# Column-tiled issue of the dense matmuls that stand between a score visit and the values after it

## Chip, cores and metric

The kernel runs on one core of one Trainium2 chip. The metric is device time in microseconds (us); lower is better. The time before is the median of three runs, 385.58 us.

## What is computed

Sigmoid attention (8 batches, 12 heads, 448 positions, head width 64) is followed by a two-layer network with a swish gate, on 3584 tokens of width 768 and a hidden width of 2048.

```python
scores = scale * np.matmul(q, k.transpose(0, 1, 3, 2)) - np.log(S)
attn = 1.0 / (1.0 + np.exp(-scores))
x = np.matmul(attn, v)              # then heads side by side: (3584, 768)
h = x @ w_in                        # (3584, 2048)
g = h * (1.0 / (1.0 + np.exp(-beta * h)))
out = g @ w_out                     # (3584, 768)
```

Inputs and output are float32; the kernel multiplies in fp16 and accumulates in float32.

## The kernel before

TensorE (PE) does four kinds of matmul, each in its own tiling of the 128 x 128 array:

- **Scores** (`score`, line 200): a contraction over 32 rows, so four matmuls stand in the array at once, each on its own 32 rows ("32*128" in the profile; "32*64" for the last 64 keys of a head). `visit(g, jt)` makes the scores of four heads (a group g, 24 in all) against the jt-th 128 keys, in 8 matmuls of 448 columns, and lets ScalarE (ACT) turn them into attention weights (`weigh`, line 211). The fourth visit (jt = 3, 64 keys) is made for two groups at once, with the odd group.
- **Values** (`attend`, line 266): the attention weights times v. A head fills 64 columns of the array, so two heads stand side by side ("128*64"), each streaming its own 448 columns. `attend` takes four heads as two slots of two: three pairs for the first slot, three for the second, then four matmuls in "64*64" for the last 64 keys. Each slot accumulates in a PSUM bank of its own, and VectorE (DVE) copies it to `xT` (line 275).
- **First layer** (`dense1`, line 284): six matmuls of the full array ("128*128") with 448 columns per 128 hidden units (224 columns in the opening part); then a sigmoid on ACT (line 292) and a product on DVE (line 295).
- **Second layer**: `dense2` (line 314) and `strassen` (line 396), full array, mostly 384 columns per matmul. `strassen` does two row tiles with seven products in place of eight; DVE adds up the products (line 415) and prepares sums of hidden values (line 385).

PE's work is laid out by hand. The main loop (line 607) goes through the visits of the groups from 3 on. After each visit a `while` loop (line 636) fills in "units" of dense work, of a list made beforehand, up to a budget; a visit and its filling are some 3 us. When the visits of a group are through, the next step of the loop begins with line 612, which fills a few more units if PSUM banks are held, and then calls `attend` for the finished group. So the order on PE around the end of a group is: last visit of group g, dense units, values of group g, first visit of group g+1, dense units, and so on. `spread`, `rest` and the units' costs decide only how many units stand in each place.

A matmul is two instructions on PE: a load of the stationary operand (PEld) and the matmul that streams the moving one. For a dense matmul the stationary operand is a 128 x 128 block (`w_in16` in the first layer, `gt` or `sums` in the second), the moving one is `xT` or a weight block, and the output is one PSUM bank, given by `bank`, which hands out the bank that has been out of use for longest.

Of the kernel before, what the change touches and what calls it, by code (L numbers as in the profile page):

```python
# [13 lines left out]
def kernel(  # L14
# [10 lines left out]
    nc = tc.nc  # L25
# [3 lines left out]
    B, H, S, D = q.shape  # L29
    NTOK, DM = out.shape  # L30
    DFF = moe_w_in.shape[1]
    P = 128
# [51 lines left out]
    def bank(name: str, cols: int = S, hold=None):  # L84
        i = min((i for i in used if i not in held.values()), key=used.get)
        touch(i)
        if hold is not None:
            held[hold] = i
        return psum["one"].tile([P, cols], FP32, tag=f"one{i}", name=name)
# [27 lines left out]
    def load_qk(g: int):  # L117
        load_one(g, 0)
        load_one(g, 1)
# [4 lines left out]
    def last_base(s: int) -> int:  # L124
        return (s % 2 ^ swapped(s // 2)) * KL
# [27 lines left out]
    def load_w_out(c: int, half: int):  # L153
# [4 lines left out]
            in_=moe_w_out[c * n * P : (c + 1) * n * P, cols].rearrange("(c p) f -> p c f", p=P),  # L158
        )

    qT = {}
    kT = {}
    at_tiles = {}
# [91 lines left out]
    def attend(g: int, c0: int, n: int, part=(0, 1)):  # L255
        b, t = divmod(g, QPB)
        if b not in xTs:
            xTs[b] = xTp.tile([P, NHC, S], FP16, tag="xT", name="xT")
        slots = [2 * g + x for x in part]
        avs = [bank("av_ps") for _ in slots]  # L260
        todo = [(s, av, jt) for s, av in zip(slots, avs) for jt in range(JF)]
        for s, av, jt in todo + [(s, av, JF) for s, av in zip(slots, avs)]:
            at = at_tiles.pop((s, jt, c0))
            base, nk = (last_base(s), KL) if jt == JF else (0, P)
            for hh in range(2):
                nc.tensor.matmul(  # L266
                    av[hh * D : (hh + 1) * D, 0:n],
                    vs[b][base : base + nk, 2 * (s % NPAIR) + hh, jt],
                    at[base : base + nk, hh, 0:n],
                    start=(jt == 0),  # L270
                    stop=(jt == JF),
                    tile_position=(base, hh * D),
                )
        for s, av in zip(slots, avs):
            nc.vector.tensor_copy(out=xTs[b][:, s % NPAIR, c0 : c0 + n], in_=av[:, 0:n])  # L275
# [4 lines left out]
    def dense1(b: int, dc: int, c0: int = 0, n: int = S):  # L280
        off = (b % 2) * S + c0
        m1 = bank("m1_ps")
        for hc in range(NHC):
            nc.tensor.matmul(  # L284
                m1[:, 0:n],
                w_in16[:, hc, dc * P : (dc + 1) * P],
                xTs[b][:, hc, c0 : c0 + n],
                start=(hc == 0),
                stop=(hc == NHC - 1),
            )  # L290
        sg = sigp.tile([P, S], FP32, tag="sg", name="sg")
        nc.scalar.activation(  # L292
            out=sg[:, 0:n], in_=m1[:, 0:n], func=AF.Sigmoid, bias=0.0, scale=beta_sb[:, dc : dc + 1]
        )
        nc.vector.tensor_tensor(  # L295
            out=gt[:, dc, off : off + n], in0=m1[:, 0:n], in1=sg[:, 0:n], op=ALU.mult
        )
# [4 lines left out]
    def release(key):  # L302
        touch(held.pop(key))
        m2s.pop(key)

    def dense2(t: int, half: int, part: int):
        last = t == NT - 1
        mid = 512 if last else HALF
        lo, hi = (0, mid) if half == 0 else (mid, DM)
        if part == 0:  # L310
            m2s[t, half] = bank("m2_ps", hi - lo, (t, half))
        m2 = m2s[t, half]
        for dc in range(part * NDC // N2, (part + 1) * NDC // N2):
            nc.tensor.matmul(  # L314
                m2,
                gt[:, dc, cols(t)],
                w_out16[:, dc, lo:hi],
                start=(dc == 0),
                stop=(dc == NDC - 1),
            )  # L320
        if part < N2 - 1:
            return
        release((t, half))
        if half == 0:
            osbs[t] = outp.tile([P, DM], FP32, tag="osb", name="osb")
        osb = osbs[t]
        nc.vector.tensor_copy(out=osb[:, lo:hi], in_=m2)  # L327
        if last:
            store(t, lo, hi)
        elif half == 1:  # L330
            store(t, 0, DM)
# [3 lines left out]
    def cols(t: int):  # L335
        return slice(t % NTILE * P, (t % NTILE + 1) * P)
# [44 lines left out]
    def hidden_sum(t: int, i: int):  # L381
        _, x, y, op, _ = product(t, i)
        if op is not None:
            sums[t, i] = sump.tile([P, ND, P], FP16, tag="sum", name="sum")
            nc.vector.tensor_tensor(out=sums[t, i], in0=x, in1=y, op=op)  # L385

    def strassen(t: int, i: int, part: int):
        name, x, _, op, w = product(t, i)
        if part == 0 and i + 2 < NPROD:
            hidden_sum(t, i + 2)  # L390
        first = (t, name) not in m2s
        if first:
            m2s[t, name] = bank("m2_ps", HALF, (t, name))
        m2 = m2s[t, name]
        for dc in range(part * ND // 2, (part + 1) * ND // 2):
            nc.tensor.matmul(  # L396
                m2,
                (x if op is None else sums[t, i])[:, dc],
                w[:, dc],
                start=first and dc == 0,  # L400
                stop=(dc == ND - 1),
                skip_group_check=i >= 4,
            )
            first = False if dc else first
        if part == 0:
            return
        if i == 0:
            for u in (t, t + 1):
                osbs[u] = outp.tile([P, DM], FP32, tag="osb", name="osb")
        L, R = slice(0, HALF), slice(HALF, DM)  # L410
        o1, o2 = osbs[t], osbs[t + 1]
        r, a = m2s.get((t, "r")), m2s.get((t, "a"))

        def add(out, in0, in1, op=ALU.add):
            nc.vector.tensor_tensor(out=out, in0=in0, in1=in1, op=op)  # L415

        if i == 1:
            nc.scalar.copy(out=o2[:, L], in_=a)
        elif i == 2:
            nc.vector.tensor_copy(out=o1[:, L], in_=m2)  # L420
            add(o1[:, R], r, o1[:, L])
            release((t, "s"))
        elif i == 3:
            add(o2[:, L], m2, o2[:, L])
            release((t, "b"))
        elif i == 4:
            add(o2[:, R], a, o2[:, L], ALU.subtract)
        elif i == 5:
            add(o2[:, R], r, o2[:, R])
            release((t, "r"))  # L430
            store(t + 1, 0, DM)
        elif i == 6:
            add(o1[:, L], a, o1[:, L], ALU.subtract)
            release((t, "a"))
            store(t, 0, DM)
# [50 lines left out]
    def fill_units(n: int):  # L486
        for _ in range(n):
            fill[at_fill[0]][2]()
            at_fill[0] += 1
# [4 lines left out]
    with tc.manual_schedule():  # L494
# [90 lines left out]
        visits = [(QPB, jt, ()) for jt in range(JF + 1)]  # L585
# [21 lines left out]
        for i, (g, jt, also) in enumerate(visits):  # L607
            if jt == 0:
                if g > QPB:


                    while len(held) > 1 and (len(held) > 2 or fill[at_fill[0]][3]):
                        spent += fill[at_fill[0]][0]
                        fill_units(1)
                    attend(g - 1, 0, S)
                if g + 2 < NQUAD:
                    if g + 2 not in raws:
                        load_qk(g + 2)
                if g + 1 < NQUAD and (g + 1) % QPB == 0:
                    load_v((g + 1) // QPB)  # L620
            visit(g, jt, also)
            if jt in (1, 2) and QPB < g < NQUAD - 1:
                transpose(g + 1, jt - 1)
            if jt == 2 and g % QPB == 0 and g > QPB:
                double_v_last(g // QPB)
            for name, part in adds.get(i, ()):
                weight_sum(name, part)
            budget += spread[i] if i < len(spread) else rest
            if (g, jt) == (QPB, JF):
                fill_units(3 * N2 // 4)  # L630
                spent += 3 * M2_US / 4
                transpose(g + 1, 0)
                transpose(g + 1, 1)
                double_v_last(1)
            goal = max(budget, spent + LEAST_US) if g > QPB + 2 else budget
            while at_fill[0] < len(fill):
                cost, ready, _, _ = fill[at_fill[0]]
                if ready > g or spent + cost / 2 > goal:
                    break
                spent += cost  # L640
                fill_units(1)
        attend(NQUAD - 1, 0, S)
        fill_units(len(fill) - at_fill[0])


# [28 lines left out]
```

## Time and profile before

| | us |
|---|---|
| three runs | 385.4, 385.58, 386.72 |
| the profiled execution | 385.93 |
| its span on the core | 384.2 |
| PE busy in the span | 377.9 |
| ACT busy | 229.3 |
| DVE busy | 231.9 |

The span runs from the first to the last instruction of the core; the other 1.7 us of the profiled execution lie around it. The granted TensorE clock was 1.0. In rows of the profile a line such as "PE L396 MATMUL ... 128*128 128x384 f16 x12" is read so: twelve matmuls of line 396 in the 128*128 tiling, with 384 columns streamed. Successive matmuls overlap, since the duration of one holds its way through the array; what one costs is the step from its start to the start of the next.

### The profile page before, as it was taken

The page shows a single profiled execution, that of the slowest core. Times are in us where ns is not written, and L with a number is a line of the kernel's source. Part 1 is how long each engine was busy: PE and PEld are TensorE (multiplying, and loading weights), DVE is VectorE, ACT ScalarE, POOL GpSimd, SP SyncE. Part 2 cuts the span into 40 slices and gives each one's busy share as a digit, 9 for nine tenths or more (in the row PEclk, how much of TensorE's full clock was granted, in tenths as well). Part 3 has the DMA queues.
Part 4 walks back from the last instruction along what each step waited for, and adds up shares of the span by engine and source line. Part 5 has one row for each costly group of instructions (what it writes and reads, how often), then busy time and mean ns, then how long its engine had stood idle before and what let it go on. Part 6 is the DMA issues. An engine that isn't in the chain of part 4 may idle for free.

```text
span 384.2 us, 7371 instructions
## 1 busy us (share of the span) xinstructions
PE 377.9 (98%) x2987; PEld 190.6 (50%) x2987; DVE 231.9 (60%) x439; ACT 229.3 (60%) x330; POOL 66.4 (17%) x114
## 2 busy tenths in 40 slices
PE   8999999999999999999999999999999999999996
PEld 3478744444544444444554445544455444555563
DVE  3347366775765557555774657665675665655761
ACT  5987856697355776487355782477752787535200
POOL 7833343140110410040110410113100000000000
PEclk9999999999999999999999999999999999999999
DMA  9999999845363930572363750649203300030033
GB/s 166 171 197 204 197 205 212 166 67 58 49 130 84 120 50 2 130 95 26 49 130 84 97 74 2 131 88 116 49 0 84 84 1 2 0 84 0 0 84 123
DMA packets 42401, 34.64 MB, mean 90 GB/s; under 512 B 21872, under 2 KB 38656, under 8 KB 42368
## 3 DMA queue, kind: packets, MB, share of 16 engines
q0 software_dynamic: 36688, 22.47, 43.1%
q1 hardware_dynamic: 5680, 11.71, 11.6%
q8 instruction: 23, 0.38, 0.4%
q14 instruction: 10, 0.08, 0.1%
HBM read 45.62 MB, written 11.01 MB: 147 GB/s over the span
## 4 chain that ended last, share of the span: by engine, by line
PE 92%; DMA 4%; POOL 1%; issue 1%; ACT 0%; DVE 0%; ACTq 0%; POOLq 0%
PE m_ps L284 38%; PE m_ps L396 29%; PE sco L200 10%; PE av_ps L266 9%; PE m_ps L314 6%; DMA w_in<-in_moe_w_in_dram 3%; DMA v<-in_v_dram 2%; POOL raw L110 1%; POOL w_in L148 1%; ACT attnT L211 0%; ACT sg L292 0%; DVE osb L327 0%; DVE gt L295 0%; POOL dummy L510 0%; ACTq L292 0%
## 5 line engine op out<-in xcount | busy, mean ns | idle before, releaser
L211 ACT ACTIVATE attnT<-sco 128x896 f16<-128x896 f32 (+1 forms) x171 | 145.1, 902 | 83.3 <-PE sco L200 82.7
L284 PE MATMUL m_ps<-xT,w_in 128*128 128x448 f16 (+1 forms) x864 | 154.7, 332 | 0.7 <-DMA w_in<-in_moe_w_in_dram 0.5
L295 DVE TENSOR_TENSOR gt<-m_ps,sg 128x448 f16<-128x448 f32 (+1 forms) x144 | 81.4, 572 | 81.3 <-ACT sg L292 77.4
L284 PEld LDWEIGHTS <-w_in 128*128 128x128 f16 x864 | 80.4, 98 | 71.5 <-issue 15.1
L292 ACT ACTIVATE sg<-m_ps,beta_sb 128x448 f32<-128x448 f32 (+1 forms) x144 | 84.1, 596 | 36.9 <-PE m_ps L284 29.9
L396 PEld LDWEIGHTS <-sum 128*128 128x128 f16 x480 | 45.2, 98 | 36.2 <-issue 7.9
L200 PE MATMUL sco<-qT,kT 32*128 32x448 f16 (+3 forms) x864 | 51.8, 340 | 0.9 <-DVE kT L186 0.7
L396 PE MATMUL m_ps<-w_T,sum 128*128 128x384 f16 x288 | 51.6, 327 | 0.0
L110 POOL DMA_DIRECT2D raw<-in_q_dram x26 | 14.3, 552 | 183.5 <-DVE kT L190 177.4
L415 DVE TENSOR_TENSOR osb<-m_ps,osb 128x384 f32<-128x384 f32 x60 | 33.3, 555 | 18.7 <-PE m_ps L396 16.9
L266 PE MATMUL av_ps<-attnT,v 128*64 128x448 f16 (+3 forms) x432 | 40.7, 340 | 0.0
L275 DVE CAST xT<-av_ps 128x448 f16<-128x448 f32 (+1 forms) x54 | 28.5, 568 | 17.8 <-PE av_ps L266 17.7
L385 DVE TENSOR_TENSOR sum<-gt 128x1024 f16<-128x1024 f16 x60 | 39.2, 679 | 0.1
L396 PE MATMUL m_ps<-w_T,gt 128*128 128x384 f16 x192 | 34.2, 326 | 0.0
L396 PE MATMUL m_ps<-w_out,sum 128*128 128x384 f16 x192 | 33.7, 326 | 0.0
L266 PEld LDWEIGHTS <-v 128*64 128x64 f16 (+1 forms) x432 | 18.8, 108 | 23.3 <-issue 16.1
L200 PEld LDWEIGHTS <-kT 32*128 32x128 f16 (+1 forms) x864 | 13.6, 96 | 28.7 <-issue 25.9
L396 PEld LDWEIGHTS <-gt 128*128 128x128 f16 x192 | 18.1, 98 | 14.7 <-issue 3.1
L314 PE MATMUL m_ps<-w_out,gt 128*128 128x384 f16 (+2 forms) x128 | 22.5, 327 | 0.0
L131 POOL DMA_DIRECT2D v<-in_v_dram x32 | 19.8, 636 | 10.7 <-DMA w_in<-in_moe_w_in_dram 6.0
L178 DVE STREAM_TRANSPOSE qT<-raw 128x448 f32<-128x448 f32 (+1 forms) x27 | 16.6, 616 | 0.8 <-DMA raw<-in_q_dram 0.7
L314 PEld LDWEIGHTS <-gt 128*128 128x128 f16 x128 | 11.9, 98 | 10.3 <-issue 3.1
(26 smaller groups left out, 95.9 us busy)
## 6 DMA issues: line engine op xcount, KB each, us to landing
out_dram<-osb SPq DMA_DIRECT2D x98, 96.0 KB, 1.9
raw<-in_k_dram POOLq DMA_DIRECT2D x23, 224.0 KB, 4.9
raw<-in_q_dram POOLq DMA_DIRECT2D x21, 224.0 KB, 3.8
v<-in_v_dram POOLq DMA_DIRECT2D x32, 144.0 KB, 6.1
w_in<-in_moe_w_in_dram POOLq DMA_DIRECT2D x8, 384.0 KB, 10.7
w_out<-in_moe_w_out_dram POOLq DMA_DIRECT2D x4, 768.0 KB, 13.7
v<-in_v_dram POOLq DMA_DIRECT2D x16, 48.0 KB, 5.9
out_dram<-osb SPq DMA_DIRECT2D x2, 384.0 KB, 2.3
```

Source lines behind the costliest of these rows:

```text
L131: nc.gpsimd.dma_start(out=vs[b][i * BLK : (i + 1) * BLK, :, 0:JF].rearrange("p h j d -> p h (j d)"), in_=rows[:, :, JF * i * D : JF * (i + ...
L200: nc.tensor.matmul(sco[base : base + nk, hh, u0 : u0 + n], kT[g][lo : lo + BLK, jt * P : jt * P + nk, e], qT[g][lo : lo + BLK, c0 : c0 + n ...
L211: nc.scalar.activation(out=at[:, :, 0:n], in_=sco[:, :, 0:n], func=AF.Sigmoid, bias=NEG_LOG_S, scale=MSCALE,)
L266: nc.tensor.matmul(av[hh * D : (hh + 1) * D, 0:n], vs[b][base : base + nk, 2 * (s % NPAIR) + hh, jt], at[base : base + nk, hh, 0:n], start ...
L275: nc.vector.tensor_copy(out=xTs[b][:, s % NPAIR, c0 : c0 + n], in_=av[:, 0:n])
L284: nc.tensor.matmul(m1[:, 0:n], w_in16[:, hc, dc * P : (dc + 1) * P], xTs[b][:, hc, c0 : c0 + n], start=(hc == 0), stop=(hc == NHC - 1),)
L292: nc.scalar.activation(out=sg[:, 0:n], in_=m1[:, 0:n], func=AF.Sigmoid, bias=0.0, scale=beta_sb[:, dc : dc + 1])
L295: nc.vector.tensor_tensor(out=gt[:, dc, off : off + n], in0=m1[:, 0:n], in1=sg[:, 0:n], op=ALU.mult)
L314: nc.tensor.matmul(m2, gt[:, dc, cols(t)], w_out16[:, dc, lo:hi], start=(dc == 0), stop=(dc == NDC - 1),)
L385: nc.vector.tensor_tensor(out=sums[t, i], in0=x, in1=y, op=op)
L396: nc.tensor.matmul(m2, (x if op is None else sums[t, i])[:, dc], w[:, dc], start=first and dc == 0, stop=(dc == ND - 1), skip_group_check= ...
L415: nc.vector.tensor_tensor(out=out, in0=in0, in1=in1, op=op)
```

## The change

Dense matmuls go through a new helper, `dense`, which issues one matmul of 128 columns, or two of 64 columns each with a tile position of (0, 0) and (0, 64). The two write the two halves of the same PSUM bank's partitions and stream the same moving operand. Which it is depends on `tiled["cols"]`. It is set to 64 (`D`) after the last visit of a group, so for the dense units between that visit and the group's values, and back to 128 (`P`) right after `attend`. Nothing else is changed: the same units in the same places, the same banks, and on ACT, DVE, POOL and SP the same instructions in the same order.

```diff
+    tiled = {"cols": P}
+
+    def dense(to, hidden, weights, **flags):
+        step = tiled["cols"]
+        for c in range(0, P, step):
+            nc.tensor.matmul(
+                to[c : c + step],
+                hidden[:, c : c + step],
+                weights,
+                **({} if step == P else {"tile_position": (0, c)}),
+                **flags,
+            )
+
@@ dense1
-            nc.tensor.matmul(
+            dense(
                 m1[:, 0:n],
@@ dense2
-            nc.tensor.matmul(
+            dense(
                 m2,
@@ strassen
-            nc.tensor.matmul(
+            dense(
                 m2,
@@ main loop
                     attend(g - 1, 0, S)
+                    tiled["cols"] = P
...
             goal = max(budget, spent + LEAST_US) if g > QPB + 2 else budget
+            tiled["cols"] = D if i + 1 == len(visits) or visits[i + 1][:2] == (g + 1, 0) else P
             while at_fill[0] < len(fill):
...
         attend(NQUAD - 1, 0, S)
+        tiled["cols"] = P
         fill_units(len(fill) - at_fill[0])
```

In the built program this holds for 428 dense matmuls in 20 stretches: 278 of 384 columns and 150 of 448. PE gets 856 instructions more (428 loads and 428 matmuls). The first values of the main loop (group 3) come after dense units that are placed before the switch is set, with nothing filled in after it, so they keep their order in 128 columns.

## Prediction

> **What bounds the kernel now.** First the page: busy shares, the granted clock, the chain that ended last.
>
> ```profile
> span 384.2 us, 7371 instructions
> PE 377.9 (98%) x2987; PEld 190.6 (50%) x2987; DVE 231.9 (60%) x439; ACT 229.3 (60%) x330; POOL 66.4 (17%) x114
> ...
> PEclk9999999999999999999999999999999999999999
> ...
> PE 92%; DMA 4%; POOL 1%; issue 1%; ACT 0%; DVE 0%; ACTq 0%; POOLq 0%
> ```
>
> The second view is all the waits of PE (engine, line, waited for: us in total, times, longest):
>
> ```profile
> PE idle_ps L520 <- DVE still L514: 1.2, 1, 1.2
> PE sco L200 <- DVE kT L186: 0.7, 1, 0.7
> PE m_ps L284 <- DMA w_in<-in_moe_w_in_dram: 0.5, 1, 0.5
> PE sco L200 <- ACT attnT L211: 0.2, 1, 0.2
> PE m_ps L284 <- DVE gt L295: 0.2, 1, 0.2
> ```
>
> PE is busy for 98% of the span, and its waits add up to 2.8 us, the last of them (after `gt`) at 47.6 us. From there on PE waits for no other engine, so a nanosecond less or more on PE in the main loop is one of the whole. But busy is not streaming. The steps from start to start show what else PE spends. The third view is the timeline of PE around the end of one group, in narrow windows (start, us, what, count):
>
> ```profile
> 201.64 0.65 PE L396 MATMUL m_ps<-w_T,sum 128*128 128x384 f16 x3
> 202.22 0.38 PE L266 MATMUL av_ps<-attnT,v 128*64 128x448 f16 x2
> ...
> 202.22 0.57 PE L266 MATMUL av_ps<-attnT,v 128*64 128x448 f16 x4
> ...
> 202.22 0.76 PE L266 MATMUL av_ps<-attnT,v 128*64 128x448 f16 x6
> ...
> 203.79 0.57 PE L200 MATMUL sco<-qT,kT 32*128 32x448 f16 x8
> 204.30 0.34 PE L396 MATMUL m_ps<-w_T,sum 128*128 128x384 f16 x1
> ...
> 204.30 0.50 PE L396 MATMUL m_ps<-w_T,sum 128*128 128x384 f16 x2
> ```
>
> Three dense matmuls of 384 columns take 0.65 us, of which the last one's own duration is 0.326: a step of 0.162, and the last starts at 201.97. The values start at 202.22, a step of 0.25 to 0.26 in place of 0.162. Read instruction by instruction, the trace gives for all steps with a change of tiling in the main loop: 384 dense to values 255 to 256 ns (ordinary 162.5), 448 dense to values 282 to 283 ns (ordinary 189), scores to dense 285 to 286 ns, dense to scores 98 ns above the ordinary step. Each change of the array's tiling costs 93 to 119 ns, whatever stands on its two sides. Within one tiling, from slot to slot of the values or from layer to layer of the dense work, there is no such step.
>
> **The change part by part.** The order before is scores (32 rows), dense (128*128), values (128*64): two changes. After, the dense work has the values' tiling, and the second change is gone. The first one stays.
>
> *Removed:* 20 stretches. 11 end on a 384-column matmul, 9 on a 448-column one (from the built order). 11 x (256 - 162.5) + 9 x (282 - 189) = 1029 + 837 = 1866 ns, **1.87 us**.
>
> *Moved:* each tiling starts with a slow second step, as the weights behind it are not loaded yet. In values the second pair starts 213 ns after the first, against 189 in the steady run (0.38, 0.57 and 0.76 for two, four and six matmuls show it to the hundredth): 24 ns too many. In dense work after scores it is 173.5 against 162.5, or 200 against 189: 11 ns. The values now go on in a running tiling and save 24; the dense stretch starts as pairs and pays, I take it, 24 instead of 11. Net 20 x (24 - 13) = 220 ns, **0.22 us**; bounds 0.1 (half the 24 stays) and 0.5 (dense pairs start as well as single ones).
>
> *Added:* 428 more loads and matmuls. No pair of dense matmuls is in the trace, but the values are such pairs: two 64-column matmuls side by side in one bank, 3 to 4 ns apart. They go at 189.0 ns per pair of 448 columns, as a single dense matmul of 448 does (189 to 190). What a pair of 384 does depends on whether two loads fit in 162 ns. The half-width values of the opening part answer that:
>
> ```profile
> 30.62 0.55 PE L266 MATMUL av_ps<-attnT,v 128*64 128x224 f16 x8
> ```
>
> Four pairs in 0.55 us, less the last matmul's 0.259 and its 3 ns: 0.288 us for three steps, 96 ns per pair, which is also what a single dense matmul of 224 columns costs (95 to 96). So two 64-column loads need at most 96 ns, below 162 and 189, and the added loads lie beside the stream. I cost them at nothing. The nearest rows above are 11 ns (the restart step of a single matmul) and 24 (that of a pair); below, the values' 189.0 against up to 189.3 on average for dense is 0.1 us over 150 pairs. What hides them is the streaming of the pair before; without that cover a pair would need two loads, 2 x 109 ns.
>
> The rows of the loads by form (busy us, mean ns, idle before):
>
> ```profile
> L396 PEld LDWEIGHTS <-sum 128*128 128x128 f16 x480 | 45.2, 98 | 36.2 <-issue 7.9
> ...
> L266 PEld LDWEIGHTS <-v 128*64 128x64 f16 x324 | 15.7, 109 | 14.6 <-issue 8.0 <-DMA raw<-in_q_dram 0.2
> ```
>
> A load of half the columns takes longer (109 against 98 ns), so it is done in a slower way. The Trainium skill (TensorEngine Tiling (Array Packing), Restrictions and Gotchas) says that column tiling excludes the fast weight load, which speaks against this change; the two durations agree with it. If the loads of a pair went one after the other, that rule would make the time the one of rival A below; the 96 ns step says they do not.
>
> *Waits:* in the built order the other engines' streams are unchanged. 22 waits of a PE instruction for PE's own count go and three come; the steps after values are 305 to 306 ns with and without such a wait, so they cost nothing either way.
>
> *What is late next:* the second slot of the values needs a bank that DVE has just read. The tightest case is after a run of `strassen` units, in 6 stretches:
>
> ```profile
> 101.61 0.55 DVE L415 TENSOR_TENSOR osb<-m_ps,osb 128x384 f32<-128x384 f32 x1
> ...
> 101.79 0.38 PE L266 MATMUL av_ps<-attnT,v 128*64 128x448 f16 x2
> ```
>
> DVE's add ends 374 ns after the values start, the second slot starts at 592 ns. After the change the values start 93 earlier against the dense work and the slot 25 earlier still: it is needed at 567 with the add ending at 374 + 93 = 467. That leaves 100 ns, and PE needs 54 from such an end (DVE's `gt` ends at 47.521, PE goes on at 47.575). So 46 ns are left: no stall.
>
> **Sum.** 1.87 + 0.22 = 2.09 us less. Against the profiled execution: 385.93 - 2.09 = 383.84. That execution stands 0.35 above the median of the runs, so as a median 385.58 - 2.09 = **383.5 us**, 0.54% less.
>
> **Rivals.**
>
> *A, the loads of a pair follow one another.* Place: every dense pair. Price: 218 ns per pair (2 x 109): 278 x (218 - 162.5) + 150 x (218 - 189) = 15.4 + 4.4 = 19.8 us, less the 2.1: 403.3. For it: the longer load rows. Against: the 96 ns pairs.
>
> *B, the shared moving operand slows the pair.* This ends on the other side. Place: the 428 pairs, where two 64-column tiles read the same addresses of SBUF 3 to 4 ns apart; values read two different halves of `attnT`, so no row shows it. It decides from 2.09 / 428 = 4.9 ns per pair on. With the 11 ns of the restart row: 4.7 us, 385.58 + 4.7 - 2.1 = 388.2. Against: the streams of two tiles are separate for values, at full rate, from one buffer. If the two took turns altogether it would be 278 x 162.5 + 150 x 189 = 73.5 us, 457.
>
> *C, part of it is given back in a wait.* If DVE's add or its signal is later than reckoned, the 6 strassen stretches lose the whole 118 ns that the second slot moves: 0.7 us, 384.2. For it: 46 ns is little. Against: PE has not waited once since 47.6 us.
>
> *D, it does not do what it says.* The 94 ns come with the first values, not with the tiling: 385.6. For it: the step has been seen only with both. Against: going from slot to slot, with new bank and weights, costs no step, and every other change of tiling costs about the same.
>
> **How the numbers follow.** Chances: forecast 0.68, A 0.05, B 0.08, C 0.12, D 0.07. The forecast's own range is 383.0 to 384.0 (0.1 to 0.5 for the restarts, and the runs' own scatter, two of which are 0.2 apart). To hold 8 in 10 the range must take in C with some scatter: 382.9 to 384.8; A, B and D, 0.20, are left out. About 0.5% (1.9 us) is what a measurement of this kernel can tell from no change, and the forecast is only 0.15 us beyond it: of its 0.68, I put 0.57 on faster and 0.11 on the same; C and D are the same (0.19); A and B are slower (0.13). Faster 0.57, same 0.30, slower 0.13.
>
> **What would show it.** 3415 matmuls in place of 2987. In the timeline after a stretch: values of 448 start 162 to 163 ns after the last 384-column pair, 189 after a 448 one, and their second pair 189 later (right). Scores to dense still 280 to 286 ns. Pairs of 384 at 162 to 163 ns: at 167 or more B has eaten the gain, near 218 it is A. If PE's list of waits has a new line for values after DVE's line 415, it is C. If the step to the values stays at 255 or 282, it is D. The prediction is wrong if the steps are as said and the time still does not fall by some 2 us.

## The result and the profile after

The changed kernel takes 383.84 us (median of 22 runs) against 385.48 us of the kernel before: ratio 0.9955, 95% interval 0.9945 to 0.9965. The ratio leaves out one run of the kernel before that took 630.38 us, and it is not quite the quotient of the two medians (0.9957); its interval leaves out 1. Two later sets of runs gave 0.9963 (0.9944 to 0.9982) and 0.9940 (0.9921 to 0.9960). The profiled execution took 383.76 us against 385.93, its span 382.0 against 384.2.

The page of the changed kernel: instructions, busy time and the chain that ended last.

```profile
span 382.0 us, 8227 instructions
...
PE 375.9 (98%) x3415; PEld 199.2 (52%) x3415; DVE 231.8 (61%) x439; ACT 229.5 (60%) x330; POOL 66.4 (17%) x114
...
PE 92%; DMA 4%; POOL 1%; issue 1%; ACT 0%; DVE 0%; ACTq 0%; POOLq 0%
```

PE has 428 matmuls more, is busy for 2.0 us less, and still bounds the kernel: the busy times of DVE, ACT and POOL are the same to 0.2 us. The weight loads (PEld) are busy for 8.6 us more, beside the matmuls. The list of PE's waits has the five entries of before and no new one; the total is 2.6 us, and the last is again the one for `gt` at 47.5 us:

```profile
PE idle_ps L533 <- DVE still L527: 1.2, 1, 1.2
PE sco L213 <- DVE kT L199: 0.5, 1, 0.5
PE m_ps L166 <- DMA w_in<-in_moe_w_in_dram: 0.5, 1, 0.5
PE sco L213 <- ACT attnT L224: 0.2, 1, 0.2
PE m_ps L166 <- DVE gt L308: 0.2, 1, 0.2
```

The timeline of PE in narrow windows, at the same place in the program as the one shown of before (start, us, what, count). `L166` is the matmul in `dense`, `L279` that of the values.

```profile
200.54 0.65 PE L166 MATMUL m_ps<-w_T,sum 128*64 128x384 f16 x6
201.03 0.36 PE L279 MATMUL av_ps<-attnT,v 128*64 128x448 f16 x2
...
201.03 0.54 PE L279 MATMUL av_ps<-attnT,v 128*64 128x448 f16 x4
...
201.03 0.73 PE L279 MATMUL av_ps<-attnT,v 128*64 128x448 f16 x6
...
202.58 0.57 PE L213 MATMUL sco<-qT,kT 32*128 32x448 f16 x8
203.09 0.34 PE L166 MATMUL m_ps<-w_T,sum 128*128 128x384 f16 x1
```

Three pairs of 384 columns take 0.65 us, as three single matmuls did. The last pair starts 0.32 after the first, at 200.87, and the values follow at 201.03: an ordinary step of 0.16, where there were 0.25 to 0.26 before. The values run through from their first pair on (0.36, 0.54, 0.73 for two, four and six, against 0.38, 0.57, 0.76). From the values to the next single dense matmul it takes 2.06 us (203.09 - 201.03), before 2.08.

All 20 stretches look like this. Read instruction by instruction:

| step on PE, ns | before | after |
|---|---|---|
| last dense 384 to first values | 255 to 256 | 162 to 163 (pair to pair) |
| last dense 448 to first values | 282 to 283 | 189 |
| first to second pair of values | 213 | 189 |
| last score to first dense of the stretch | 285 to 286 | 282 to 284 |
| first to second dense after it, 384 / 448 | 173 / 200 | 186 / 213 (pairs) |
| dense 384 / 448, steady | 162.5 / 189 | 162.5 / 189 (pairs and singles) |

The loads show what else is different at the step: before, the first load for the values begins with the values, at 202.22, after 0.32 us in which no load ran; with the change the values' loads begin at 200.87, beside the last dense pair. The rows are of before and then of the changed kernel:

```profile
202.22 0.11 PEld L266 LDWEIGHTS <-v 128*64 128x64 f16 x2 [0.32 <-issue]
```

```profile
200.87 0.28 PEld L279 LDWEIGHTS <-v 128*64 128x64 f16 x4
```

From the first values of group 3 (51.39 us before, 51.35 after) to the first values of group 23 (336.09 and 333.94) it takes 284.70 us before and 282.59 after: **2.11 us less**. That interval starts with the first values of the main loop and holds all 20 stretches. Its ends, before and then with the change:

```profile
51.39 0.38 PE L266 MATMUL av_ps<-attnT,v 128*64 128x448 f16 x2
336.09 0.38 PE L266 MATMUL av_ps<-attnT,v 128*64 128x448 f16 x2
```

```profile
51.35 0.38 PE L279 MATMUL av_ps<-attnT,v 128*64 128x448 f16 x2
333.94 0.36 PE L279 MATMUL av_ps<-attnT,v 128*64 128x448 f16 x2
```

### The profile page after: what moved, and what is told of

Same layout as the page of the kernel before. It is cut to its first block, busy times and chain, and to the rows that moved or that the text cites. A ratio compares the mean times of both kernels' runs of the same rounds, so it can differ in the third digit from the quotient of the medians.

```text
span 382.0 us, 8227 instructions
## 1 busy us (share of the span) xinstructions
PE 375.9 (98%) x3415; PEld 199.2 (52%) x3415; DVE 231.8 (61%) x439; ACT 229.5 (60%) x330; POOL 66.4 (17%) x114
## 4 chain that ended last, share of the span: by engine, by line
PE 92%; DMA 4%; POOL 1%; issue 1%; ACT 0%; DVE 0%; ACTq 0%; POOLq 0%
PE m_ps L166 73%; PE sco L213 10%; PE av_ps L279 9%; DMA w_in<-in_moe_w_in_dram 3%; DMA raw<-in_k_dram 2%; POOL raw L110 1%; POOL w_in L148 1%; ACT attnT L224 0%; ACT sg L305 0%; DVE osb L340 0%; DVE gt L308 0%; POOL dummy L523 0%; ACTq L305 0%; POOLq L674 0%
## 5 line engine op out<-in xcount | busy, mean ns | idle before, releaser
L166 PE MATMUL m_ps<-xT,w_in 128*128 128x448 f16 (+2 forms) x1014 | 154.7, 336 | 0.7 <-DMA w_in<-in_moe_w_in_dram 0.5
L166 PEld LDWEIGHTS <-w_in 128*128 128x128 f16 (+1 forms) x1014 | 82.8, 101 | 69.3 <-issue 15.1
L166 PEld LDWEIGHTS <-sum 128*64 128x64 f16 (+1 forms) x664 | 48.1, 104 | 33.5 <-issue 7.9
L166 PE MATMUL m_ps<-w_T,sum 128*128 128x384 f16 (+1 forms) x360 | 51.6, 327 | 0.0
L166 PEld LDWEIGHTS <-gt 128*128 128x128 f16 (+1 forms) x414 | 31.4, 103 | 23.8 <-issue 6.2
L279 PE MATMUL av_ps<-attnT,v 128*64 128x448 f16 (+3 forms) x432 | 40.2, 338 | 0.0
L288 DVE CAST xT<-av_ps 128x448 f16<-128x448 f32 (+1 forms) x54 | 28.5, 567 | 15.3 <-PE av_ps L279 14.3
L166 PE MATMUL m_ps<-w_T,gt 128*64 128x384 f16 (+1 forms) x268 | 34.3, 327 | 0.0
L166 PE MATMUL m_ps<-w_out,sum 128*64 128x384 f16 (+1 forms) x304 | 33.8, 327 | 0.0
L279 PEld LDWEIGHTS <-v 128*64 128x64 f16 (+1 forms) x432 | 20.6, 108 | 18.8 <-issue 9.2
L166 PE MATMUL m_ps<-w_out,gt 128*128 128x384 f16 (+3 forms) x146 | 22.6, 327 | 0.0
L431 ACT COPY osb<-m_ps 128x384 f32<-128x384 f32 x12 | 5.8, 481 | 16.8 <-PE m_ps L166 16.8
```

Source lines behind the costliest of these rows:

```text
L166: nc.tensor.matmul(to[c : c + step], hidden[:, c : c + step], weights, **({} if step == P else {"tile_position": (0, c)}), **flags,)
L279: nc.tensor.matmul(av[hh * D : (hh + 1) * D, 0:n], vs[b][base : base + nk, 2 * (s % NPAIR) + hh, jt], at[base : base + nk, hh, 0:n], start ...
```

## The experiments

*Theory T*: a change of the array's tiling costs some 94 ns of PE wherever it stands, a pair costs no more than a single matmul, and the gain is the 20 changes saved. *Rival D* (of the prediction): the step belongs to the values, not to the tiling. *Rival B*: the shared moving operand makes pairs slower. *Rival K* was formed on the result, since the timed runs show somewhat less (1.6 us) than the trace: pairs draw the granted clock below 1.0 in some runs.

A trace places a difference better than a time does here, as said below, so each measurement names the interval from the first values of group 3 to those of group 23 too ("the loop"; 284.70 us before, 282.59 with the change).

**The changed kernel again** (`e1_after_again`, and `e8_after_third` in a later set).

> The changed kernel again, beside the same runs of the kernel before as the next three. Theory T (a change of the array's tiling costs some 94 ns of TensorE, pairs cost nothing): 2.1 us less than before, 383.4 where before is 385.5, ratio 0.9946, granted clock 1.0 in all runs as often as for before. Rival K (pairs of 64 columns pull the granted clock below 1.0 in some runs, so 428 of them give back some 0.35 us of the 2.1): ratio 0.9955, with a granted clock of 0.998 or 0.999 in about a third of the runs, and fewer such runs for before.

> The changed kernel once more, on the chip of the two before it. Theory T: ratio 0.9946 as its trace has it. If something outside the traced execution takes part of the gain: 0.9955 to 0.9963 again.

Measured: ratios 0.9963 (0.9944 to 0.9982) and 0.9940 (0.9921 to 0.9960); the loop took 282.60 us in both traces. The loop is the same to 0.01 us, while the times scatter. Among the ten traces the reason is the opening part: in these kernels, which are the same up to there but for one stretch in one of them, the first score of 448 columns started between 36.19 and 37.16 us. That is half of the change's size. The traces part mainly at the first score (5.74 to 6.16 us), which waits for `kT`, and in the dense stretch that begins at about 22 us (1.8 to 2.5 us long), where in some of them PE waits for a load of `w_in`. Runs without a trace don't show where they lost time. The longer ones tend to have a lower granted clock: in the first set the 13 runs of the changed kernel at a clock of 1.0 have a median of 383.62 us, the 4 below 0.999 one of 384.82. The ratios lie on both sides of the trace's 0.9946 (2.1 of 385.5).

**All dense matmuls from the main loop on as pairs** (`e2_all_pairs`, again as `e7_all_pairs_again`):

```diff
                     attend(g - 1, 0, S)
-                    tiled["cols"] = P
+                    tiled["cols"] = D
...
-            tiled["cols"] = D if i + 1 == len(visits) or visits[i + 1][:2] == (g + 1, 0) else P
+            tiled["cols"] = D
...
         attend(NQUAD - 1, 0, S)
-        tiled["cols"] = P
+        tiled["cols"] = D
```

> All dense matmuls from the second visit of group 3 on are issued as pairs, up to the end: 1544 pairs in place of 428; one change of tiling fewer than the changed kernel has (202 against 203). Theory T: the pairs' steps are those of single matmuls; 54 more stretches start as pairs (24 ns instead of 11), less some 2 ns at each entry, so +0.6 us against the changed kernel, less 0.1: ratio to before 0.996, 384.0. Rival K: the loss grows with the pairs, 0.35 x 1544 / 428 = 1.3 us, so 385.0 to 385.4 and a granted clock below 0.999 in most runs. Rival B of the prediction (11 ns per pair): +12 us.

> All dense matmuls of the main loop as pairs again, for the granted clock. Theory T: 384.2, ratio 0.996, and no lower a clock than for the changed kernel. Rival K: the clock is below 0.999 in more runs than for the changed kernel, since it has 3.6 times its pairs.

Measured: 384.17 us, ratio 0.9954 (0.9936 to 0.9972), and 383.93, 0.9945 (0.9925 to 0.9965). The loop took 283.24 and 283.25 us, 0.65 more than with the change (its ends in `e2_all_pairs`):

```profile
51.38 0.36 PE L279 MATMUL av_ps<-attnT,v 128*64 128x448 f16 x2
334.62 0.35 PE L279 MATMUL av_ps<-attnT,v 128*64 128x448 f16 x2
```

The first-layer row by form, 448 columns (busy us, mean ns), of this kernel and then of before:

```profile
L166 PE MATMUL m_ps<-xT,w_in 128*64 128x448 f16 x1344 | 134.8, 354 | 0.0
```

```profile
L284 PE MATMUL m_ps<-xT,w_in 128*128 128x448 f16 x672 | 134.2, 353 | 0.0
```

Twice the matmuls, 0.6 us more busy; streamed one after the other they would have taken twice the time. What is left in the loop is the slower start of the stretches: 50 more of them start as pairs, at 13 ns each 0.65 us. Rival B falls for 1544 pairs, whose widths go from 224 to 512 columns. Rival K does not hold as it was put: with 3.6 times the pairs the granted clock was below 0.999 in 1 of 12 runs, and the 385.0 to 385.4 us that it asked for did not come. For the changed kernel the clock was that low in 9 of 46 runs, for the one before in 3 of the 46 whose clock is on record. Why, and whether by more than chance, is not settled, but it doesn't grow with the number of pairs.

**Pairs everywhere but ahead of values** (`e3_pairs_elsewhere`):

```diff
-            tiled["cols"] = D if i + 1 == len(visits) or visits[i + 1][:2] == (g + 1, 0) else P
+            tiled["cols"] = P if i + 1 == len(visits) or visits[i + 1][:2] == (g + 1, 0) else D
```

> The condition turned round: pairs (868) in the dense stretches that do not stand before values, single matmuls in those that do. 222 changes of tiling, one fewer than before. Theory T: no gain, 54 stretches with the slower start, 54 x 11 = 0.6 us, less 0.1: 386.0, ratio 1.001. If pairs as such were what helps (not the change of tiling that they save): below 385.5, by up to 2 x 2.1 us. Rival K: 0.7 us on top of T, 386.7, with lower granted clocks.

Measured: 386.33 us, ratio 1.0019 (1.0004 to 1.0034); the loop 285.35 us, 0.65 more than before:

```profile
51.22 0.35 PE L279 MATMUL av_ps<-attnT,v 128*64 128x448 f16 x2
336.57 0.38 PE L279 MATMUL av_ps<-attnT,v 128*64 128x448 f16 x2
```

So 868 pairs bring nothing by themselves and cost their slower starts. The two halves add up: -2.11 for the pairs ahead of values and +0.65 for the others make -1.46, and all pairs together took 284.70 - 283.24 = 1.46 less.

**The first unit of each stretch single** (`e4_first_unit_whole`). The values still follow pairs, but the change of tiling lies inside the dense work:

```diff
-            tiled["cols"] = D if i + 1 == len(visits) or visits[i + 1][:2] == (g + 1, 0) else P
+            ends = i + 1 == len(visits) or visits[i + 1][:2] == (g + 1, 0)
             while at_fill[0] < len(fill):
...
                 fill_units(1)
+                if ends:
+                    tiled["cols"] = D
```

> As the changed kernel, but the first unit (4 or 6 matmuls) of each of the 20 stretches stays single, the others are pairs (332). The values still follow pairs, but the change of tiling now lies inside the stretch: 223 changes as before. Theory T: all of the gain goes, ratio 1.000, 385.5. If the step belonged to the values after single matmuls (D of the prediction) and not to the tiling: 383.4 to 383.9 as with the change.

Measured: 385.55 us, ratio 0.9994 (0.9975 to 1.0012); the loop 284.72 us, that of before to 0.02. The timeline in narrow windows shows the ends of the loop and where the step went: the last single matmul and the first pair of one product, then the last pairs and the values.

```profile
50.68 0.38 PE L279 MATMUL av_ps<-attnT,v 128*64 128x448 f16 x2
...
198.66 0.33 PE L166 MATMUL m_ps<-w_out,sum 128*128 128x384 f16 x1
...
198.91 0.35 PE L166 MATMUL m_ps<-w_out,sum 128*64 128x384 f16 x2
...
200.88 0.82 PE L166 MATMUL m_ps<-w_T,sum 128*64 128x384 f16 x8
201.53 0.36 PE L279 MATMUL av_ps<-attnT,v 128*64 128x448 f16 x2
...
335.40 0.35 PE L279 MATMUL av_ps<-attnT,v 128*64 128x448 f16 x2
```

Two matmuls of the same product, into the same bank, are 0.25 apart where 0.16 is ordinary; what differs is that the second is one of a pair. The step into the values is ordinary: the four pairs start at 200.88, the last of them three steps of 0.16 later at 201.37, and the values 0.16 after that. The step goes where the change of tiling goes, so rival D falls.

**Single and paired units in turn** (`e5_alternate`), in the stretches that don't stand before values:

```diff
+            ends = i + 1 == len(visits) or visits[i + 1][:2] == (g + 1, 0)
+            tiled["cols"] = D if ends else P
...
                 fill_units(1)
+                if not ends:
+                    tiled["cols"] = D if tiled["cols"] == P else P
```

> As the changed kernel, but in the dense stretches that do not stand before values the units go in turn as single matmuls and as pairs: 136 changes of tiling more (76 into pairs, 60 out of them), 768 pairs. Theory T with the measured steps: 76 x (93 + 24) + 60 x (96 + 11) = 15.3 us more than the changed kernel, some 399, ratio to before 1.034. If a change costs only where values or scores are on one side: as the changed kernel with some slower starts, 384 to 385.

Measured: 398.62 us, ratio 1.0328 (1.0306 to 1.0350), 15.2 us above the 383.41 of the changed kernel, which ran beside it; 15.3 were expected. In the trace the loop grew by 13.2 us against the changed kernel, and the piece from the first 448-column score to the values of group 3, where the rest of the changes lie, by 1.6: 14.8 us for 136 changes, 109 ns each with the slower start behind it. The timeline in narrow windows, into a pair and out of it:

```profile
211.76 0.33 PE L166 MATMUL m_ps<-w_T,sum 128*128 128x384 f16 x1
...
212.02 0.35 PE L166 MATMUL m_ps<-w_T,sum 128*64 128x384 f16 x2
...
212.53 0.33 PE L166 MATMUL m_ps<-w_T,sum 128*64 128x384 f16 x2
...
212.79 0.34 PE L166 MATMUL m_ps<-w_T,sum 128*128 128x384 f16 x1
```

0.26 in both directions, where 0.16 is ordinary; no score and no values are near.

**Two more stretches as pairs** (`e6_two_more`): before the last values of the opening part and before those of group 3.

```diff
+                if (g, second) == (QPB - 1, 1):
+                    tiled["cols"] = D
                 fill_units(g if second else 2 + g)
         fill_units(1)
         attend(QPB - 1, QH, QH)
+        tiled["cols"] = P
...
+                tiled["cols"] = D
                 fill_units(3 * N2 // 4)
```

> The changed kernel with pairs also in the two stretches that it leaves out (before the last values of the opening part, and before those of group 3): 201 changes of tiling, 458 pairs. Theory T: 2 x 0.1 us less than the changed kernel, so 2.3 us less than before in a trace, which is less than the runs can tell; 383.3 to 383.7. Rival K: no lower than the changed kernel.

Measured: 383.5 us, ratio 0.9928 (0.9915 to 0.9942), the loop 282.57 us. The two steps into the values are ordinary there (96 ns for 224 columns in place of 189, 162 for 384 in place of 256). But in this trace PE then waited at 43 us for the load of `w_out`, and the matmul behind it came 0.37 us later than in step (in `e1_after_again` the same matmul came 0.22 late, for which the list of waits has no entry), so that the 0.2 us expected did not reach the values of group 3. It is the lowest ratio measured, but the 383.41 us of the changed kernel beside it, and the scatter of the runs, don't let the runs tell the two apart.

## Why the prediction was right

- **Forecast**: 2.09 us less, 383.5. The trace has 2.11 us in the loop (and another 24 ns in the last values, behind the interval's end); the median of the runs is 383.84, 0.34 above the forecast and inside its range. The gap is of the size of the scatter of the runs: three sets gave -1.7, -1.4 and -2.3 us (ratios times 385.5), while the traced loop repeats to 0.01. What each run lost, in the opening part or by its clock, is not known.
- **The changes saved** (1.87): 20 steps of 93 to 94 ns, as forecast. Moving the change (`e4_first_unit_whole`) and adding 136 (`e5_alternate`) show that the tiling is the cause. The Trainium skill (TensorEngine Tiling (Array Packing), Tiling Modes) says that a change of the mode drains TensorE; the steps fit it and price it at 93 to 98 ns for most pairs of modes, 114 to 117 on leaving 64*64. Counted by the ordinary steps, the prediction's 98 ns for dense to scores is 96 (258 against 162.5, 285 against 189), and its upper end of 119 is 117; neither is in the sum.
- **The slow starts** (0.22): values saved 24 each, dense stretches paid 13 more each, both as taken. The start of the dense pairs had been a guess from the values' row, and it came out. The reason given, that the weights behind the first pair are not loaded yet, is not shown by itself: the first pair of a tiling lasts 24 to 25 ns longer than the later ones (350 against 326 ns at 384 columns), its own loads begin only with it, and the loads behind it some 26 ns after it rather than 2. Not foreseen were 2 to 3 ns less at the entry from scores, some 0.05 us in 20 stretches, which is what the trace has beyond the forecast.
- **The pairs at nothing**: right for every width tried. The rule of the Trainium skill that the prediction weighed (TensorEngine Tiling (Array Packing), Restrictions and Gotchas), that column tiling excludes the fast weight load, fits the durations: 110 ns for the 64-column loads of dense work against 98 for 128 columns. In the steady steps the longer loads cost nothing, since two of them lie side by side. The row of the changed kernel's loads by form shows it:

```profile
L166 PEld LDWEIGHTS <-sum 128*64 128x64 f16 x368 | 20.4, 110 | 10.5 <-issue 1.9
```

  Busy time counts overlap once: 20.4 us for 368 loads is 55 ns per load, half of its own duration. The prediction's 0.1 us for the steps of 448 columns is 0.05 by its own figures, 0.3 ns over 150 pairs; it is not in the sum.
- **The bank of the second slot** (rival C): in the tight case DVE's add ended 473 to 477 ns after the values' start and the slot began at 567 to 568, where 467 and 567 were forecast. PE didn't wait:

```profile
101.27 0.55 DVE L428 TENSOR_TENSOR osb<-m_ps,osb 128x384 f32<-128x384 f32 x1
...
101.34 0.92 PE L279 MATMUL av_ps<-attnT,v 128*64 128x448 f16 x8
```

  The first slot has three pairs. Four take 0.92 us: three ordinary steps of 0.19 and the last one's own 0.35, so the fourth, the first of the second slot, came in step.
- **The chances**: the forecast stood 0.15 us beyond the bound of 0.5%, and the first set's ratio, 0.45% less, came to lie just inside that bound, the third set's beyond it. That the same had 0.30 came for its larger part from rivals C and D, which did not happen; the scatter of the runs did.

## What to carry to other kernels

Where TensorE is the bound and changes between tilings, count the changes: each costs 93 to 98 ns here, and 114 to 117 on leaving 64*64, and the kernel before makes 223 of them (without those around the idle matmuls at the start). A full-array matmul could be issued as two column halves at no extra TensorE time at every width tried, 224 to 512 columns; shorter streams, which might not cover the loads, were not run. So work that stands beside a tiled stage can take on that stage's tiling; halves that save no change only bring slower starts. And an effect of half a per cent is read better from the same stretch in two traces than from times, when a part that varies from run to run stands ahead of it.

## What was not expected

- The change of tiling costs about the same inside one accumulation into one bank, between two matmuls that differ only in their columns (255 ns from start to start at 384 columns, of which 162.5 are the stream).
- Two column halves of a dense matmul that stream the same moving operand 3 to 4 ns apart go at the step of one full matmul, at 224 (96 ns per pair), 384 (162.5) and 448 columns (189).
- In three traces of the changed kernel the opening part took 36.22, 36.91 and 37.11 us, while the 282.6 us of the loop repeated to 0.01.
